# A float16 score pass over 64 rows widened to 128 with zeros, the weight split taken off GpSimd, and a new order

## The chip, the cores and the metric

The kernel runs on one core of one Trainium2 chip. The metric is the device time of one execution in microseconds; the kernel before has a median of 1103.67 us over 3 runs (1102.92 to 1103.91). The engines have short names in the profile: PE is the matrix engine and PEld its weight loads, DVE is VectorE, ACT is ScalarE, POOL is GpSimd, SP is the engine whose queue issues the DMAs.

## The reference

Block-causal attention over 8 batches of 8 heads (576 tokens, head size 64), then a feed-forward layer on the 4,608 tokens with 512 features, 2,048 hidden. All arrays are float32.

```python
scores = scale * np.matmul(q, k.transpose(0, 1, 3, 2))
mask = block_i >= block_j                  # blocks of 64 tokens
scores = np.where(mask, scores, -1000000000.0)
scores = scores - np.max(scores, axis=-1, keepdims=True)
attn = np.exp(scores)
attn = attn / (np.sum(attn, axis=-1, keepdims=True) + 1e-09)
out = np.matmul(attn, v)
...
h = x @ w_in
g = np.maximum(0.01 * h, h)
return (g @ w_out).astype(np.float32)
```

## The kernel before, in words

**Precision.** To reach float32 accuracy at the speed of 16-bit matmuls, an operand is split into a high half (the value scaled by a power of two and rounded to float16) and a low half (what is left over). A product then takes several matmuls that add up in one accumulator. The powers of two come from sums of squares: one per weight matrix, one per group of four heads for v and for q and k, one per stretch of x.

**Stages.** `work` lists 80 pieces of attention. Batch 0 comes as 8 "lo" and 8 "hi" pieces with float32 matmuls, while both weight matrices are loaded, their squares summed and then split; batch 1 comes as 8 "first" and 8 "rest" pieces; all further heads are "full". From batch 3 on (`SB = 3`), 40 heads in all, the scores are computed in float16 (`sixteen`). The feed-forward work goes by 18 chunks of 256 tokens, each with 8 units of two matmul groups: `ffn1` (line 989, 24 matmuls a unit, result through ScalarE's leaky step and split into `gh` and `gl`) and `ffn2` (line 1007, 12 matmuls a unit). A chunk becomes available when the attention of its tokens is done.

**The float16 scores** (lines 537 to 551 and 590 to 595). q and k of a head lie in `qk_in` with 128 rows: the 64 features and, below, the 64 features again in reverse roles. Four steps make the operands. ScalarE or VectorE writes `sx2`, the scaled high half of k, and the upper half of `sx1`, the high half of q. VectorE's line 546 writes `sx3`, what `sx2` left over; its upper 64 rows are the low half of k, its lower 64 rows the low half of q. Two DMAs of 72 KB each on SP, both within the on-chip memory, bring q's low half under q's high half (line 549) and k's high half a second time under itself (line 550). The first matmul pass, over 128 rows, then multiplies q's high and low halves by k's high half at once; the second, over 64 rows, multiplies q's high half by k's low half:

```python
nc.tensor.matmul(
    ap, sx1[0:64, cols] if c else sx1[:, cols], sx3[0:64, k0:k1] if c else sx2[:, k0:k1], start=first, stop=last
)
```

A head has two blocks of such matmuls at line 591. The first has the query tiles in the order (3, 0), (0, 0), (3, 1), (0, 1), (2, 0), (1, 0), (2, 1), (1, 1), where the second number is the pass; their widths are 448, 64, 448, 64, 320, 192, 320 and 192 columns. The second block, for tile 4, has two matmuls of pass 0 and two of pass 1, 288 columns each. The maxima (line 622), the exponentials (line 639), the split of the probabilities (lines 682 and 686), their transposes by DMA (line 693) and the values (line 809) follow. The buffers of a head alternate between two sets, so a head's operands can be made while the head before is at work, but not before the scores two heads back are done.

**The weight split** (`weight_split`, lines 464 to 486). When all 16 pieces of a matrix are loaded and the scale is known, each piece of 128 x 512 gets a high half by ScalarE, VectorE or GpSimd and a low half by VectorE or GpSimd. GpSimd takes two instructions for a low half (lines 475 and 476).

**What sets the order.** Nothing is scheduled on the chip. `Plan` is a list scheduler that runs while the kernel is built: every operation has a rank, mostly in units of one head, one or more engines with a cost in ns for each, and the buffers that it reads and writes. The planner replays time with those costs, gives each free engine the ready operation of the lowest rank, and the instructions are emitted in that order. On the chip every engine, SP's queue included, runs its own list in order and waits where an operand is not there. The constants of lines 39 to 84 shift the ranks: `OFF1`, `OFF2`, `SL1` and `AHEAD` place the weight pieces and their loads, `LEAD` and `LAG` the feed-forward units behind the attention, `RP` the making of a head's operands, `RN` the split of the probabilities. `HOLD` and `HOLDP` are delays after which the second choice of engine is considered. `fill` puts dummy matmuls on PE in the first stage.

Of the kernel before, what the change touches and what calls it, by code (L numbers as in the profile page):

```python
# [12 lines left out]
F16 = mybir.dt.float16  # L13
BF16 = mybir.dt.bfloat16
AF = mybir.ActivationFunctionType
ALU = mybir.AluOpType
# [6 lines left out]
S = 576  # L23
# [12 lines left out]
GROUP = 4  # L36
AHEADV = 3
AHEADQ = 5
RW = -0.799

RL = 4.591
RP = -0.92
RB = 0.202
RT = 2.998
RV = 2.189
RX = -6.219
RN = -1.606

LEAD = 3.83
LAG = 1.993  # L50
RS = 2.699
RG = 0.188
OFF1 = 4.299
OFF2 = -4.211
SL1 = 12.694
AHEAD = -2.515

LAT = 1550
HOLDP = 475.817
HOLD = 186.808  # L60
FILL = 235
FILLTO = 12
# [12 lines left out]
TISSUE, TMOVE = 1230, 125  # L75
SLOW = 8000
SIDE = 34
STEPA = 0.586
STEPB = 0.594
VD = 4.394  # L80
JOINT = 0
SB = 3
RQ = 3.331
RD = 0.704


class Plan:
# [148 lines left out]
def dma(size):  # L236
    return size / 360


def pool2(n):  # L240
    return n * 2.14 + 168


def pool1(n):
    return n * 0.83 + 240
# [3 lines left out]
def attention_ffn(ctx: ExitStack, tc: tile.TileContext, qk0: bass.AP, qk: bass.AP, v: bass.AP, w_in: bass.AP, w_out: bass.AP, out: bass.AP):  # L249
    nc = tc.nc  # L250
# [10 lines left out]
    add = plan.add  # L261
# [67 lines left out]
    ptf = fixed([P, 1024], F32, "ptf")  # L329
# [36 lines left out]
    def carve(y, shape, dt):  # L366
        size = 1
        for n in shape:
            size *= n
        words = size // (1 if dt == F32 else 2)  # L370
        ap = slab[y][:, used[y] : used[y] + words].bitcast(dt)
        used[y] += words
        if len(shape) == 1:
            return ap
        names = "abcd"[: len(shape)]
        return ap.rearrange(f"p ({' '.join(names)}) -> p {' '.join(names)}", **dict(zip(names[1:], shape[1:])))
# [4 lines left out]
    xr[1] = carve(0, [ND, S], F32)  # L381
    ob[1] = carve(0, [DM], F32)
    xh[1], xl[1] = (carve(1, [ND, CH], F16) for _ in range(2))
    qk16 = [carve(y, [3, S], F16) for y in range(2)]
    prow = [prow, [carve(1, [pw[t]], F32) for t in range(NT)]]

    def powers(e, s, i):
# [76 lines left out]
    def weight_split(rank, f, out_side):  # L464
        w, y = WIDE, 1 if out_side else 0
        if out_side:
            hi, lo = woh[:, f], wol[:, f]
        else:
            hi, lo = (x[:, f].rearrange("p c f -> p (c f)") for x in (wih, wil))
        key, v_key = ("wo" if out_side else "wi", f), ("val", out_side, f)  # L470
        val = slab[y][:, f * WIDE : (f + 1) * WIDE].bitcast(F32)
        by = ws[:, y : y + 1]

        def twice():
            nc.gpsimd.tensor_scalar(val, val, by, 1.0, op0=ALU.mult, op1=ALU.mult)
            nc.gpsimd.tensor_sub(lo, val, hi)  # L476

        add([
            ("ACT", act(w, True) + 93, lambda: nc.scalar.mul(hi, val, by)),
            ("POOL", pool1(w), lambda: nc.gpsimd.tensor_scalar(hi, val, by, 1.0, op0=ALU.mult, op1=ALU.mult)),  # L480
            ("DVE+", dve(w, True), lambda: nc.vector.tensor_scalar_mul(hi, val, by)),
        ], rank, [v_key, ("ws", y)], [(key, 0)])
        add([
            ("DVE+", dve(w) + 62, lambda: nc.vector.scalar_tensor_tensor(lo, val, by, hi, op0=ALU.mult, op1=ALU.subtract)),
            ("POOL", pool1(w) + pool2(w), twice),
        ], rank, [v_key, (key, 0), ("ws", y)], [(key, 1), v_key])

    def attention(i):
        n, kind = work[i]
        b, h = divmod(n, H)  # L490
        z = i % 2
# [3 lines left out]
        qkt, qkey = qk_in[z], ("qkt", z)  # L495
# [38 lines left out]
        rp = r0 - RP  # L534
        if plain_s:
            qkd = [qkey]
        elif sixteen:
            eq, kq = divmod(n - SB * H, GROUP)
            sx1, sx2, sx3 = (qk16[z][:, y] for y in range(3))
            c = 2 * GROUP * eq + kq  # L540
            mine, cross = later["qsc"][:, c : c + 1], later["qsc"][:, c + GROUP : c + GROUP + 1]
            esc = later["qx"][:, GROUP * eq + kq : GROUP * eq + kq + 1]
            k1, k2, k3 = (("x", z, y, "q") for y in range(3))
            add(copying(S, lambda: sx2, lambda: qkt[:, 1], by=cross), rp, [qkey, ("qsc", eq)], [k2])
            add(copying(S, lambda: sx1[0:64], lambda: qkt[0:64, 0], by=mine[0:64]), rp, [qkey, ("qsc", eq)], [k1])
            add([("DVE+", dve(S) + 120, lambda: nc.vector.scalar_tensor_tensor(
                sx3, qkt[:, 1], cross, sx2, op0=ALU.mult, op1=ALU.subtract
            ))], rp, [qkey, ("qsc", eq), k2], [k3])
            add([("SP", 475, lambda: nc.sync.dma_start(sx1[64:128], sx3[64:128]))], rp, [k3], [k1], lag=dma(S * 64 * 2))
            add([("SP", 475, lambda: nc.sync.dma_start(sx2[64:128], sx2[0:64]))], rp, [], [k2], lag=dma(S * 64 * 2))  # L550
            qkd = [k1, k2, k3]
        else:
            qd, khd, kld = qs[z][:, qa:qe], kk[z][:, 0, :ke], kk[z][:, 1, :ke]
            add(copying(qe - qa, lambda: qd, lambda: q_in, by=eighth[:, 0:1]), rp, [qkey], [("qs", z)])
            add(copying(ke, lambda: khd, lambda: k_in, by=eighth[:, 1:2]), rp, [qkey], [("kh", z)])
            add(subtracting(qe - qa, lambda: qd[64:128], lambda: q_in[64:128], lambda: qd[64:128]), rp, [qkey], [("qs", z)])
            add(subtracting(ke, lambda: kld[0:64], lambda: k_in[0:64], lambda: khd[0:64]), rp, [qkey, ("kh", z)], [("kl", z)])
            qkd = [("qs", z), ("kh", z), ("kl", z)]
        if not plain_v:
            e, k = divmod(n - H, GROUP)  # L560
            vkey, by, back = ("vr", e % 2, k), vsc[:, e : e + 1], vin[:, e : e + 1]
# [17 lines left out]
        def scores(tiles):  # L579
            banks = [bank for bank, _ in tiles]  # L580
            for y, (b, (t, ap, k0, k1, c)) in enumerate(tiles):
                first, last = b not in banks[:y], b not in banks[y + 1 :]
                cols = slice(q0[t], q0[t] + P)
                if plain_s:
                    go = lambda ap=ap, cols=cols, k0=k0, k1=k1, first=first, last=last: nc.tensor.matmul(
                        ap, q_in[:, cols.start - qa : cols.stop - qa], k_in[:, k0:k1], start=first, stop=last
                    )
                    yield 4 * RATE * (k1 - k0), go, LOADS
                    continue
                if sixteen:  # L590
                    go = lambda ap=ap, cols=cols, k0=k0, k1=k1, c=c, first=first, last=last: nc.tensor.matmul(  # L591
                        ap, sx1[0:64, cols] if c else sx1[:, cols], sx3[0:64, k0:k1] if c else sx2[:, k0:k1], start=first, stop=last
                    )
                    yield RATEH * (k1 - k0), go, LOADH
                    continue
                if c == 2:
                    go = lambda ap=ap, cols=cols, k0=k0, k1=k1, first=first, last=last: nc.tensor.matmul(
                        ap, qs[z][:, cols], kk[z][:, :, k0:k1], start=first, stop=last
                    )
                    yield 2 * RATE * (k1 - k0), go, LOADS  # L600
                    continue
                go = lambda ap=ap, cols=cols, c=c, k0=k0, k1=k1, first=first, last=last: nc.tensor.matmul(
                    ap, qs[z][:, cols], kk[z][:, c, k0:k1], start=first, stop=last
                )
                yield RATE * (k1 - k0), go, LOADS
# [129 lines left out]
        for base, c0, w, items in tgroups.get(kind, ()):  # L735
            x = bank()
# [7 lines left out]
            hi = ptf[:, base : base + w]  # L744
# [141 lines left out]
    def q_group(e):  # L886
# [4 lines left out]
        if e == 0:  # L891

            def blocks():
                for ap, x in ((same, 0), (other, 64)):
                    nc.gpsimd.memset(ap, 0.0)
                    nc.gpsimd.memset(ap[0:64, x : x + 64], 1.0)
                    nc.gpsimd.memset(ap[64:128, 64 - x : 128 - x], 1.0)

            add([("POOL", 1200, blocks)], rank - 2, [], [("ptf", 0), ("ptf", 512), "blocks"])
        for k in range(GROUP):  # L900
            y = (GROUP * e + k) % 3
            buf, key = q_raw[y], ("qn", y)
# [137 lines left out]
    for i in range(len(work) + 1):  # L1040
        if i == 2 * H:

            def second(y):
                nc.gpsimd.memset(parts[y], 0.0)

            for y in range(2):
                new = [("ph", y, t, k) for t in range(NT) for k in (0, 1)] + [("pt", y, t) for t in range(NT)]
                new += [("p", 1, t) for t in range(NT)] + [(a, 1, d) for a in ("xh", "xl") for d in range(0, CH, BLK)] if y else [("x", 1, h, k) for h in range(H) for k in range(3)] + [("ob", 1)]
                new += [("x", y, k, "q") for k in range(3)]
                kind = "wo" if y else "wi"  # L1050
                add([("POOL", 2500, lambda y=y: second(y))], 0, [("val", bool(y), f) for f in range(NF)], new)
        if i in events:
# [63 lines left out]
```

## Time and profile before

| | |
|---|---|
| median of 3 runs | 1103.67 us |
| the profiled execution | 1104.85 us, span 1103.0 us |
| mean granted clock of PE | 0.986 |
| PE busy | 1064.6 us (97%) |
| VectorE, ScalarE, GpSimd busy | 64%, 66%, 16% |
| line 591, score matmuls in float16 | 480 matmuls, 349.7 to 922.0 us |
| DMAs from `slab` to `slab`, 72 KB each | 80 |

The profile shows one execution. A group row names line, engine, operation, output<-inputs, shapes and count; then busy us, the mean ns of one, and the engine's idle time before the group with what ended it. A timeline row begins with start and length in us; `[x <-y]` at its end is idle time before it and the releaser. Rows of stages give the stretch, its length, busy us and instruction counts of PE, PEld, DVE, ACT and POOL (of those that have any), the granted clock as a share of full speed, the busy share of the DMA engines and GB/s. Matmuls are pipelined: a matmul's printed length overlaps the next, so what a run of matmuls takes is read from start to start. SPq is SP's queue of DMA issues.

### The profile page before, as it was taken

How to read it: one execution, taken by the hardware profiler on the slowest of the kernel's cores; microseconds unless marked ns; L12 is line 12 of the kernel's file. 1: busy time of each engine (PE TensorE's matmuls, PEld its weight loads, DVE VectorE, ACT ScalarE, POOL GpSimd, SP SyncE). 2: the span in 40 equal slices, each digit the busy share in tenths (PEclk: the TensorE clock that was granted, in tenths of full speed). 3: DMA queues.
4: the chain of work that ended last, by engine and by line, in shares of the span. 5: the costliest groups of instructions: out<-in, count | busy, mean ns of one | idle time of the engine just before them, and what ended most of it. 6: DMA issues, size and time to landing. Idle time of an engine off the chain costs nothing.

```text
span 1103.0 us, 22107 instructions
## 1 busy us (share of the span) xinstructions
PE 1064.6 (97%) x8374; PEld 737.4 (67%) x8374; DVE 702.6 (64%) x1861; ACT 723.9 (66%) x1687; POOL 181.1 (16%) x224
## 2 busy tenths in 40 slices
PE   9999799998897899999999999999999999999998
PEld 7887466676664566666666666666666666766665
DVE  4687556888888777786866576676666765221111
ACT  5888546777886777786766577788767765322222
POOL 1010610431442210222100002211121210000000
PEclk9999899999999799999999999999999999999999
DMA  7856235798789787778884756878776754000000
GB/s 267 269 172 235 70 90 110 133 203 185 183 195 219 165 184 159 150 160 194 151 171 83 168 150 135 166 166 176 127 169 126 144 86 92 1 20 4 17 21 19
DMA packets 263178, 152.56 MB, mean 138 GB/s; under 512 B 223648, under 2 KB 240032, under 8 KB 263072
## 3 DMA queue, kind: packets, MB, share of 16 engines
q1 hardware_dynamic: 263072, 151.16, 59.7%
q8 instruction: 65, 1.06, 0.4%
q14 instruction: 41, 0.34, 0.1%
HBM read 80.74 MB, written 9.44 MB: 82 GB/s over the span
## 4 chain that ended last, share of the span: by engine, by line
PE 66%; DVE 1%; DMA 1%; ACT 0%; issue 0%; SPq 0%; DVEq 0%
PE p_h L989 27%; PE p_o L1007 26%; PE p_s L591 6%; PE p_t L809 5%; DMA slab<-slab 1%; PE p_t L952 0%; PE p_t L913 0%; DVE nm L622 0%; PE p_t L880 0%; ACT prow L639 0%; DVE slab L686 0%; DVE xl L973 0%; DVE xh L969 0%; DVE slab L1023 0%; ACT slab L1022 0%
## 5 line engine op out<-in xcount | busy, mean ns | idle before, releaser
L989 PEld LDWEIGHTS <-wih 128*128 128x128 f16 x2304 | 222.0, 99 | 74.4 <-issue 10.9
L994 ACT ACTIVATE g<-p_h 128x512 f32<-128x512 f32 x144 | 85.5, 594 | 176.4 <-PE p_h L989 172.3
L989 PE MATMUL p_h<-slab,wih 128*128 128x256 f16 x1152 | 197.2, 273 | 0.1
L1007 PE MATMUL p_o<-wol,gh 128*128 128x512 f16 x576 | 172.4, 381 | 5.6 <-POOL wol L476 5.6
L1007 PE MATMUL p_o<-woh,gh 128*128 128x512 f16 x576 | 172.9, 382 | 0.0
L1007 PE MATMUL p_o<-woh,gl 128*128 128x512 f16 x576 | 172.3, 381 | 0.0
L1007 PEld LDWEIGHTS <-gh 128*128 128x128 f16 x1152 | 109.3, 100 | 85.2 <-issue 5.8
L989 PE MATMUL p_h<-xh,wih 128*128 128x256 f16 x576 | 158.7, 276 | 2.9 <-DVE xh L969 2.9
L989 PE MATMUL p_h<-xl,wih 128*128 128x256 f16 x576 | 158.5, 275 | 1.0 <-DVE xl L973 1.0
L989 PE MATMUL p_h<-xh,wil 128*128 128x256 f16 x576 | 158.4, 275 | 0.0
L989 PE MATMUL p_h<-slab,wil 128*128 128x256 f16 x576 | 157.4, 273 | 0.0
L275 DVE TENSOR_TENSOR gl<-g,gh 128x512 bf16<-128x512 f32 x94 | 64.6, 688 | 145.4 <-ACT gh L265 122.5
L622 DVE TENSOR_REDUCE nm<-p_s 128x1 f32<-128x192 f32 (+4 forms) x308 | 138.6, 485 | 8.1 <-ACT prow L639 2.6
L989 PEld LDWEIGHTS <-wil 128*128 128x128 f16 x1152 | 113.3, 98 | 15.3 <-issue 1.6
L1007 PEld LDWEIGHTS <-gl 128*128 128x128 bf16 x576 | 56.6, 98 | 74.3 <-issue 7.0
L276 POOL TENSOR_TENSOR gl<-g,gh 128x512 bf16<-128x512 f32 x50 | 62.6, 1253 | 245.9 <-ACT gh L265 166.0
L809 PEld LDWEIGHTS <-vs 128*128 128x128 f16 x1680 | 86.0, 99 | 15.2 <-issue 9.8
L809 PE MATMUL p_t<-slab,vs 128*128 128x128 f16 (+1 forms) x1680 | 91.1, 212 | 3.4 <-DVE slab L686 1.9
L591 PE MATMUL p_s<-slab 128*128 128x448 f16 (+2 forms) x480 | 85.1, 281 | 5.0 <-ACT prow L639 2.8
L686 DVE SCALAR_TENSOR_TENSOR slab<-slab,rec 128x192 f16<-128x192 f32 (+4 forms) x140 | 76.8, 571 | 9.0 <-ACT slab L682 8.5
L686 DVE SCALAR_TENSOR_TENSOR slab<-prow,rec,slab 128x192 f16<-128x192 f32 (+4 forms) x140 | 74.4, 554 | 9.9 <-ACT slab L682 9.4
L613 DVE MEMSET p_s<- 64x64 f32 (+1 forms) x196 | 24.7, 126 | 87.6 <-PE p_s L591 55.2
(163 smaller groups left out, 1578.8 us busy)
## 6 DMA issues: line engine op xcount, KB each, us to landing
qk_in<-in_qk SPq DMA_DIRECT2D x56, 576.0 KB, 4.9
raw<-in_qk SPq DMA_DIRECT2D x40, 288.0 KB, 3.6
raw<-in_w_in SPq DMA_DIRECT2D x16, 512.0 KB, 4.6
raw<-in_w_out SPq DMA_DIRECT2D x16, 512.0 KB, 4.7
slab<-slab SPq DMA_DIRECT2D x80, 72.0 KB, 4.5
out<-ob SPq DMA_DIRECT2D x18, 256.0 KB, 2.3
out<-slab SPq DMA_DIRECT2D x18, 256.0 KB, 2.0
v_raw<-in_v SPq DMA_DIRECT2D x7, 640.0 KB, 5.3
```

Source lines behind the costliest of these rows:

```text
L275: ("DVE+" if sb else "DVE", dve(n) + 100, lambda: nc.vector.tensor_sub(dst(), one(), two())),
L276: ("POOL", pool2(n) - (0.25 * n if n == 512 else 0), lambda: nc.gpsimd.tensor_sub(dst(), one(), two())),
L591: go = lambda ap=ap, cols=cols, k0=k0, k1=k1, c=c, first=first, last=last: nc.tensor.matmul(ap, sx1[0:64, cols] if c else sx1[:, cols], sx ...
L613: nc.vector.memset(ap, NEG)
L622: [("DVE", dve(kw[t]), lambda t=t, ap=ap, flat=flat: nc.vector.tensor_reduce(nm[z][: qn[t], t : t + 1], ap[: qn[t]], axis=AX.X if flat els ...
L686: ("DVE+", dve(w) + 62, lambda: nc.vector.scalar_tensor_tensor(part(1), p, by, part(0), op0=ALU.mult, op1=ALU.subtract)),
L809: nc.tensor.matmul(p_t[x][:, c : c + src.free_size()], vs[z][:, (j + 1) % NT], src, start=start, stop=stop)
L989: nc.tensor.matmul(hh[:, i, :], w[:, f, d, :], x[:, d, :], start=k == 0, stop=k == len(terms) - 1)
L994: add([("ACT", act(512), lambda: nc.scalar.activation(g[z], hh, AF.Prelu, alpha=0.01, scale=DOWN))], rank, [("h", z)], [("g", z)])
L1007: nc.tensor.matmul(p_o[m], a[:, i, m * P : (m + 1) * P], w[:, 2 * u + i, :], start=u == 0 and k == 0, stop=u == NU - 1 and k == 5,)
```

## The change

The subtraction writes a fourth tile, `sx4`. A third DMA of the same size brings its upper 64 rows, k's low half, to `sx3[0:64]`; the lower 64 rows of `sx3` are set to zero once by GpSimd, for both sets of buffers, in the operation that also prepares the block matrices for the scales. The second pass multiplies all 128 rows of `sx1` by `sx3`, so that q's low half meets zeros. The scores' matmuls wait for all three DMAs. GpSimd is no longer a choice for either half of the weights. Nineteen of the planner's constants have other values; `LAG`, `RL`, `RS`, `HOLD`, `FILL` and the planner's costs are as before.

```diff
-RW = -0.799
+RW = -0.819
...
-RP = -0.92
-RB = 0.202
-RT = 2.998
-RV = 2.189
-RX = -6.219
-RN = -1.606
-
-LEAD = 3.83
+RP = -1.361
+RB = 0.283
+RT = 1.774
+RV = 2.243
+RX = -5.633
+RN = -1.756
+
+LEAD = 4.283
...
-RG = 0.188
-OFF1 = 4.299
-OFF2 = -4.211
-SL1 = 12.694
-AHEAD = -2.515
+RG = 0.245
+OFF1 = 4.515
+OFF2 = -4.38
+SL1 = 16.003
+AHEAD = -0.135
...
-HOLDP = 475.817
+HOLDP = 475.007
...
-STEPA = 0.586
-STEPB = 0.594
-VD = 4.394
+STEPA = 0.659
+STEPB = 0.675
+VD = 4.498
...
-RQ = 3.331
-RD = 0.704
+RQ = 3.122
+RD = 1.397
...
-    qk16 = [carve(y, [3, S], F16) for y in range(2)]
+    qk16 = [carve(y, [4, S], F16) for y in range(2)]
...
-        def twice():
-            nc.gpsimd.tensor_scalar(val, val, by, 1.0, op0=ALU.mult, op1=ALU.mult)
-            nc.gpsimd.tensor_sub(lo, val, hi)
-
         add([
             ("ACT", act(w, True) + 93, lambda: nc.scalar.mul(hi, val, by)),
-            ("POOL", pool1(w), lambda: nc.gpsimd.tensor_scalar(hi, val, by, 1.0, op0=ALU.mult, op1=ALU.mult)),
             ("DVE+", dve(w, True), lambda: nc.vector.tensor_scalar_mul(hi, val, by)),
         ], rank, [v_key, ("ws", y)], [(key, 0)])
         add([
             ("DVE+", dve(w) + 62, lambda: nc.vector.scalar_tensor_tensor(lo, val, by, hi, op0=ALU.mult, op1=ALU.subtract)),
-            ("POOL", pool1(w) + pool2(w), twice),
         ], rank, [v_key, (key, 0), ("ws", y)], [(key, 1), v_key])
...
             add([("DVE+", dve(S) + 120, lambda: nc.vector.scalar_tensor_tensor(
-                sx3, qkt[:, 1], cross, sx2, op0=ALU.mult, op1=ALU.subtract
-            ))], rp, [qkey, ("qsc", eq), k2], [k3])
-            add([("SP", 475, lambda: nc.sync.dma_start(sx1[64:128], sx3[64:128]))], rp, [k3], [k1], lag=dma(S * 64 * 2))
+                sx4, qkt[:, 1], cross, sx2, op0=ALU.mult, op1=ALU.subtract
+            ))], rp, [qkey, ("qsc", eq), k2], [k4])
+            add([("SP", 475, lambda: nc.sync.dma_start(sx1[64:128], sx4[64:128]))], rp, [k4], [k1], lag=dma(S * 64 * 2))
             add([("SP", 475, lambda: nc.sync.dma_start(sx2[64:128], sx2[0:64]))], rp, [], [k2], lag=dma(S * 64 * 2))
+            add([("SP", 475, lambda: nc.sync.dma_start(sx3[0:64], sx4[0:64]))], rp, [k4], [k3], lag=dma(S * 64 * 2))
             qkd = [k1, k2, k3]
...
                 if sixteen:
                     go = lambda ap=ap, cols=cols, k0=k0, k1=k1, c=c, first=first, last=last: nc.tensor.matmul(
-                        ap, sx1[0:64, cols] if c else sx1[:, cols], sx3[0:64, k0:k1] if c else sx2[:, k0:k1], start=first, stop=last
+                        ap, sx1[:, cols], (sx3 if c else sx2)[:, k0:k1], start=first, stop=last
                     )
...
+                for y in range(2):
+                    nc.gpsimd.memset(qk16[y][64:128, 2], 0.0)
+
-            add([("POOL", 1200, blocks)], rank - 2, [], [("ptf", 0), ("ptf", 512), "blocks"])
+            add([("POOL", 1200, blocks)], rank - 2, [], [("ptf", 0), ("ptf", 512), "blocks", ("x", 0, 2, "q"), ("x", 1, 2, "q")])
```

More of the change, by code (lines that the diff above doesn't have):

```diff
@@ L538, in attention @@
             eq, kq = divmod(n - SB * H, GROUP)
-            sx1, sx2, sx3 = (qk16[z][:, y] for y in range(3))
+            sx1, sx2, sx3, sx4 = (qk16[z][:, y] for y in range(4))
             c = 2 * GROUP * eq + kq
@@ L542, in attention @@
             esc = later["qx"][:, GROUP * eq + kq : GROUP * eq + kq + 1]
-            k1, k2, k3 = (("x", z, y, "q") for y in range(3))
+            k1, k2, k3, k4 = (("x", z, y, "q") for y in range(4))
             add(copying(S, lambda: sx2, lambda: qkt[:, 1], by=cross), rp, [qkey, ("qsc", eq)], [k2])
@@ L1048, in attention_ffn @@
                 new += [("p", 1, t) for t in range(NT)] + [(a, 1, d) for a in ("xh", "xl") for d in range(0, CH, BLK)] if y else [("x", 1, h, k) for h in range(H) for k in range(3)] + [("ob", 1)]
-                new += [("x", y, k, "q") for k in range(3)]
+                new += [("x", y, k, "q") for k in range(4)]
                 kind = "wo" if y else "wi"
```

## The prediction

> **What bounds the kernel now.** I read the page's head first, then a table of busy time by stage, then the matrix engine's own timeline and its waits.
>
> ```profile
> span 1103.0 us, 22107 instructions
> ...
> PE 1064.6 (97%) x8374; PEld 737.4 (67%) x8374; DVE 702.6 (64%) x1861; ACT 723.9 (66%) x1687; POOL 181.1 (16%) x224
> ```
>
> The stages, with PE, PEld, DVE, ACT and POOL busy, then the granted clock, DMA share and GB/s:
>
> ```profile
> 0.00:120.00 120.00, 117.81 (x886) 96.50 (x887) 86.26 (x235) 95.06 (x224) 12.34 (x32) 1.00 0.69 233
> 120.00:150.00 30.00, 24.41 (x119) 13.32 (x118) 13.96 (x37) 13.14 (x34) 17.32 (x13) 0.89 0.11 28
> 150.00:262.00 112.00, 109.85 (x896) 80.42 (x894) 85.45 (x226) 77.26 (x189) 28.77 (x29) 1.00 0.72 148
> 262.00:375.00 113.00, 90.00 (x740) 64.18 (x740) 96.62 (x260) 85.03 (x215) 35.37 (x43) 0.91 0.85 193
> 375.00:922.00 547.00, 545.30 (x4487) 363.12 (x4483) 384.85 (x1047) 401.31 (x944) 87.01 (x110) 1.00 0.71 149
> 922.00:1103.00 181.00, 177.19 (x1258) 119.88 (x1256) 35.48 (x60) 52.10 (x86) 0.32 (x1) 1.00 0.07 21
> ```
>
> From 375 us on, PE is idle for 1.7 of 547 us and then only at the end, while VectorE and ScalarE are busy 70 and 73%. In that stretch whatever PE stops doing comes off the end. The real holes are two: 120 to 150 us, with 5.6 us idle and a clock of 0.89, and 262 to 375 us, with 23.0 us idle and 0.91.
>
> **The full-row second pass.** The 40 float16 heads run two blocks of score matmuls each (line 591): eight matmuls, then four. Beside them stands a block of 30 value products (line 809), all over 128 rows.
>
> ```profile
> 571.56 1.35 PE L591 MATMUL p_s<-slab 128*128 128x448 f16 x8
> 572.84 0.39 PE L989 MATMUL p_h<-slab,wih 128*128 128x256 f16 x2
> ...
> 578.06 1.57 PE L809 MATMUL p_t<-slab,vs 128*128 128x64 f16 x30
> 579.47 0.76 PE L591 MATMUL p_s<-slab 128*128 128x288 f16 x4
> 580.16 0.39 PE L989 MATMUL p_h<-slab,wih 128*128 128x256 f16 x2
> ```
>
> Start to start is what a block costs, since the printed length overlaps the next. By the code, the value block streams 3,200 columns (20 matmuls of 128, 10 of 64); it takes 579.47 - 578.06 = 1.41 us, or 0.441 ns a column, with a new weight load for each. The eight score matmuls stream 2 x (448 + 64 + 320 + 192) = 2,048 columns, which at that rate is 0.90 us; they take 572.84 - 571.56 = 1.28 us, 0.38 too much. The four stream 4 x 288 = 1,152, worth 0.51 us, and take 0.69, 0.18 too much. Where does it go? The weight loads of the first block show it:
>
> ```profile
> 571.34 0.31 PEld L591 LDWEIGHTS <-slab 128*128 128x128 f16 x2
> 571.87 0.11 PEld L591 LDWEIGHTS <-slab 64*128 64x128 f16 x2 [0.21 <-issue]
> 572.19 0.11 PEld L591 LDWEIGHTS <-slab 128*128 128x128 f16 x2 [0.21 <-issue]
> 572.51 0.11 PEld L591 LDWEIGHTS <-slab 64*128 64x128 f16 x2 [0.21 <-issue]
> 572.84 0.11 PEld L989 LDWEIGHTS <-wih 128*128 128x128 f16 x2 [0.21 <-issue]
> ```
>
> The loader pauses each time the number of rows changes, 128 to 64 and 64 to 128, and not between equals. That makes four changes in the block of eight and two in the block of four: 0.38/4 = 95 ns and 0.18/2 = 90 ns a change, the same price twice. With 128 rows in both passes there is no change left. The columns stay as many, so the zeros cost nothing by the value block's rate. How many heads lie where this counts:
>
> ```profile
> 349.00:375.00 26.00, 5.11 (x24) 1.78 (x24) 0.74 0.89 204
> 375.00:922.00 547.00, 79.74 (x456) 31.24 (x456) 1.00 0.71 149
> ```
>
> 456 of the 480 matmuls, 38 heads, run where PE has no slack: 38 x (0.38 + 0.18) = 21.3 us. Two heads lie in a stage where PE also waits for others; I count nothing for them, and the upper bound is 40 x 0.56 = 22.4.
>
> The Trainium skill ("TensorE: Matmul & The Clock Gate", Part 3: Packing small matmuls) speaks against this: it says a weight load overlaps a running matmul only when the row groups differ. The trace disagrees, since the 30 loads of the value block, all on the same 128 rows, cost nothing.
>
> **The third copy.** SP issues two small copies per head now. The rows are those of two heads, the landing times, and PE's one wait for them:
>
> ```profile
> 558.45 0.59 SPq L550 DMA_DIRECT2D slab<-slab  x1
> ...
> 569.76 0.59 SPq L550 DMA_DIRECT2D slab<-slab  x1
> ```
>
> ```profile
> L550 SPq DMA_DIRECT2D slab<-slab x40: 467/587/695, 343.3 to 900.7; - x40
> DMA to landing us min/median/max: 2.1/4.4/7.2
> ```
>
> ```profile
> PE p_s L591 <- DMA slab<-slab: 1.7, 1, 1.7
> ```
>
> The copy issued at 558.45 feeds the block at 571.56, so it lands at about 562.9, 8.7 us early. A third behind it starts 0.59 us later and still lands some 8 us early. Queued behind it on SP are that head's neighbours' transposes and loads, each 0.59 us later. One head of 40 waited (1.7 us); it would wait 0.6 more. Its own conditions are those of the first copy (the same subtraction, the same scores two heads back), so SP does not newly wait. I take 0; the bounds are 0 and 0.6 us for each of 40 heads, 24 us, were SP's order the limit everywhere. Below zero it cannot go: it adds work only. The subtraction now writes a fourth tile, which frees VectorE from waiting for old scores; the same instruction, 0. The two zero fills on GpSimd, once, resemble this row and by their ranks lie ahead of the first float16 head, 0:
>
> ```profile
> 3.50 0.57 POOL L321 MEMSET kk<- 64x576 f32 x1
> ```
>
> **No GpSimd in the weight split.** GpSimd now does four low halves and one high half. This is the burst after the last weight piece:
>
> ```profile
> 120.54 7.35 POOL L475 TENSOR_SCALAR slab<-slab,ws 128x512 f32<-128x512 f32 x1
> 127.97 1.15 POOL L476 TENSOR_TENSOR wol<-slab,woh 128x512 f16<-128x512 f32 x1
> 129.10 0.69 POOL L475 TENSOR_SCALAR slab<-slab,ws 128x512 f32<-128x512 f32 x1
> ```
>
> ```profile
> 120.62 6.70 DVE L484 SCALAR_TENSOR_TENSOR wol<-slab,ws,woh 128x512 f16<-128x512 f32 x10
> ```
>
> ```profile
> 122.78 0.59 PE L1007 MATMUL p_o<-woh,gh 128*128 128x512 f16 x2
> 123.21 0.38 PE L1007 MATMUL p_o<-wol,gh 128*128 128x512 f16 x1
> 129.17 0.59 PE L1007 MATMUL p_o<-wol,gh 128*128 128x512 f16 x1 [5.58 <-POOL wol L476]
> ```
>
> A scaling that takes 0.69 us alone took 7.35 while VectorE ran ten splits without a pause, and ended 0.6 us after the last. PE stood 5.58 us for one low half. The Trainium skill ("SBUF — State Buffer", SBUF: two separate sides) calls the port that the two engines share an exclusive lock; this agrees. Then the clock, by the last but two number:
>
> ```profile
> 129.00:130.00 1.00, 0.83 (x3) 0.28 (x3) 0.00 (x0) 0.00 (x0) 0.92 (x3) 0.50 0.00 0
> 133.00:134.00 1.00, 1.00 (x4) 0.42 (x3) 0.00 (x0) 0.00 (x0) 1.00 (x1) 0.50 0.00 0
> 134.00:135.00 1.00, 1.00 (x6) 0.39 (x4) 0.00 (x0) 0.00 (x0) 0.26 (x1) 0.82 0.00 0
> ```
>
> From 129.17 to about 134.4, 5.2 us of matmuls ran at half clock, so 2.6 us were lost. Together 5.58 + 2.6 = 8.2 us. What replaces it: VectorE does three more splits in this burst at 6.70/10 = 0.67 us, 2.0 us. PE's pass over a pair of pieces has 12 matmuls, 2.6 us by the first two rows (two matmuls in 0.43), and needs two splits, 1.34 us; VectorE stays ahead and I take none of the 2.0. Behind it VectorE sits idle anyway:
>
> ```profile
> 137.53 0.30 DVE L613 MEMSET p_s<- 64x64 f32 x2 [10.08 <-PE p_s L585]
> ```
>
> PE is then next to continuously busy to 262 us, so the 8.2 us pass on. Bounds: 8.2, and 6.2 if the extra splits were on the path.
>
> **The order.** Nineteen constants of the planner move. By the code, the load of the first weight piece gets rank 5.15 instead of 7.21 and that of the last 20.65 instead of 19.51; preparing a float16 head is 0.44 of a head later, the feed-forward 0.45 later. No row prices this. It cannot gain from 375 us on, where PE has no holes; what it can touch are the holes before. Bounds: half of the 23.0 idle us of 262 to 375 gone, 11.5 us, or one more stall like the 8.2 us one and half as much again, 12 us. Nothing says which, so 0.
>
> **Sum.** The profiled execution took 1104.85 us (span 1103.0, 1.85 around it): 1104.85 - 21.3 - 8.2 = 1075.3. The median of the runs is 1.18 lower, 1103.67, so 1074.2, said as 1074.
>
> **Rivals.** (1) The new order closes holes: 1074 - 12 = 1062. For it: from 262 to 375 us PE, VectorE and ScalarE are busy 80, 86 and 75%, none of them full. Against: each head's chain of scores, exponentials, transposes and values stays as it is. (2) The new order opens a hole: 1074 + 12 = 1086. [...] (3) The loss is the loader's own, not the change of rows, so the passes gain nothing: 1103.67 - 8.2 = 1095.5. Against it: the loads without a pause between equal rows. (4) Slower: the third copy ends last. It decides from the point where it lands over 8 us later than I place it, for instance behind a transpose that SP holds; every microsecond beyond that is paid by each of 38 heads, and from 29.5/38 = 0.8 us on it eats the gain. At 1 us it gives 1074 + 38 = 1112. Against it: one wait in 40 now. (5) Every load of full rows waits for the running matmul as the changes do now, 12 waits a head for 6: 1103.67 - 8.2 + 38 x 6 x 0.094 = 1117. Against it: the value block's 30 loads. This is what the page named above in the Trainium skill would have.
>
> **Numbers.** Forecast 0.60, (1) 0.17, (2) 0.15, (3) 0.03, (4) 0.03, (5) 0.02. Leaving out the last three and the outer edges of (1) and (2), the range is 1061 to 1087. This kernel's measurement can tell about 0.2%, 2.2 us, from no change. Faster: all but (4) and (5), 0.94 after 0.01 for ending level; slower 0.05.
>
> **What would show it.** In the changed profile: line 591 has 480 matmuls of 128 rows, the blocks start to start 0.90 and 0.50 us, the loader without pauses of 0.2; no GpSimd under the splits and no wait of line 1007 for it; PEclk without the dip near 130 us; from the start of the float16 heads to the last some 21 us shorter; the tail's 181 us unchanged. Wrong if the blocks still take 1.28 us, if line 591 waits for the small copies in many heads, or if the idle time before 375 us differs by over 12 us.

## The result, and the profile after

The changed kernel takes 1073.12 us (median of 5 runs, 1072.22 to 1074.84) against 1103.67: a ratio of 0.972, with a 95% interval of 0.9701 to 0.974. The forecast was 1074. Its profiled execution took 1072.31 us, span 1070.2.

The same stages as before the change, with busy us of PE, PEld, DVE, ACT and POOL, the granted clock, the DMA share and GB/s:

```profile
0.00:120.00 120.00, 116.41 (x867) 94.82 (x868) 87.52 (x239) 95.15 (x225) 5.59 (x26) 1.00 0.69 233
120.00:150.00 30.00, 29.77 (x180) 18.67 (x178) 19.55 (x67) 16.98 (x47) 8.56 (x10) 1.00 0.19 48
150.00:262.00 112.00, 107.69 (x883) 77.82 (x881) 86.89 (x223) 79.28 (x186) 27.76 (x28) 1.00 0.72 159
262.00:375.00 113.00, 91.80 (x763) 68.39 (x764) 95.77 (x259) 83.13 (x207) 38.78 (x46) 0.88 0.86 186
375.00:922.00 547.00, 545.61 (x4684) 392.57 (x4683) 388.62 (x1048) 402.72 (x951) 92.15 (x121) 1.00 0.74 156
922.00:1070.00 148.00, 143.96 (x985) 96.08 (x982) 22.70 (x32) 38.29 (x62) 0.00 (x0) 1.00 0.04 15
```

Two rows differ in kind. From 120 to 150 us PE is now busy for 29.77 of 30 us, where it was 24.41, and the clock is 1.00, not 0.89. From 375 to 922 us PE is as full as it was, but 4,684 matmuls fit where 4,487 did. The hole from 262 to 375 us is as it was: 21.2 idle us and a clock of 0.88.

PE's timeline at two score blocks (line 591 is line 586 now, 602 is 597, 809 is 804, 1007 is 1004):

```profile
573.31 0.65 PE L586 MATMUL p_s<-slab 128*128 128x288 f16 x4
573.80 0.38 PE L1004 MATMUL p_o<-woh,gh 128*128 128x512 f16 x1
...
585.88 1.04 PE L586 MATMUL p_s<-slab 128*128 128x448 f16 x8
586.75 1.57 PE L804 MATMUL p_t<-slab,vs 128*128 128x64 f16 x30
```

And the loads of the block of eight, from the timeline of PEld:

```profile
585.66 0.97 PEld L586 LDWEIGHTS <-slab 128*128 128x128 f16 x8
586.67 0.29 PEld L804 LDWEIGHTS <-vs 128*128 128x128 f16 x5
```

Start to start the blocks take 0.49 and 0.87 us, where they took 0.69 and 1.28. The eight loads are one row without a pause inside it, where four rows each began with 0.21 us of idle time.

PE's waits that bear on the prediction:

```profile
PE p_s L597 <- ACT prow L634: 7.2, 7, 1.7
PE p_s L597 <- ACT slab L634: 6.7, 4, 3.0
PE p_t L804 <- DMA slab<-slab: 4.3, 3, 2.8
PE p_s L586 <- ACT prow L634: 2.6, 1, 2.6
```

The wait of 5.6 us for GpSimd's low half has no row any more, and line 586 has none for a DMA: no head waits for the small copies. The waits for ScalarE's exponentials, 12.4 us before at the float32-type scores (the two rows of line 602 together), are 13.9. From 262 to 375 us they are 10.4 of the 21.2 idle us, 11.9 of 23.0 before: about half of the hole that stays. The rest of it is spread over shorter waits for DMAs, ScalarE and VectorE.

### The profile page after: what moved, and what is told of

Its sections match the earlier page's. It is cut to its first block, busy times and chain, and to the rows that moved or that the text cites. A ratio compares the mean times of both kernels' runs of the same rounds, so it can differ in the third digit from the quotient of the medians.

```text
span 1070.2 us, 22133 instructions
## 1 busy us (share of the span) xinstructions
PE 1035.2 (97%) x8352; PEld 748.3 (70%) x8352; DVE 701.0 (66%) x1863; ACT 715.5 (67%) x1676; POOL 172.8 (16%) x231
## 4 chain that ended last, share of the span: by engine, by line
PE 65%; DMA 2%; DVE 0%; ACT 0%; issue 0%; SPq 0%
PE p_h L986 27%; PE p_o L1004 27%; PE p_t L804 5%; PE p_s L586 5%; DMA slab<-slab 1%; DMA raw<-in_qk 1%; PE p_t L949 0%; PE p_t L910 0%; ACT prow L634 0%; DVE nm L617 0%; DVE xl L970 0%; PE p_t L875 0%; DVE xh L966 0%; DVE slab L681 0%; ACT slab L1019 0%
## 5 line engine op out<-in xcount | busy, mean ns | idle before, releaser
L986 PEld LDWEIGHTS <-wih 128*128 128x128 f16 x2304 | 224.4, 99 | 70.1 <-issue 2.9
L681 DVE SCALAR_TENSOR_TENSOR slab<-prow,rec,slab 128x448 f16<-128x448 f32 (+4 forms) x140 | 74.8, 560 | 14.0 <-ACT slab L677 13.3
L586 PE MATMUL p_s<-slab 128*128 128x448 f16 (+2 forms) x480 | 69.4, 282 | 4.4 <-ACT prow L634 2.6
L265 ACT CAST gh<-g 128x512 f16<-128x512 f32 x112 | 68.9, 615 | 2.5
```

The costliest lines, as they stand in the source:

```text
L265: one = lambda: nc.scalar.copy(dst(), src())
L986: nc.tensor.matmul(hh[:, i, :], w[:, f, d, :], x[:, d, :], start=k == 0, stop=k == len(terms) - 1)
```

## The experiments

Two theories were at stake. Mine: the gain is 21 to 23 us from six changes of rows a head at some 95 ns each, and 8 us from GpSimd's late low half; the third copy and the order bring nothing. The rivals: the price lies in each 64-row matmul and not in the change; the order is the real gain; the third copy takes something back; the hole only moves. The runs are put beside the kernel before on the same chip (1102.4 to 1104.4 us) and beside the changed kernel's 1073.12. These medians of the kernel before lie 2 us apart, so a difference of under 2 us from the changed kernel is not resolved.

### The second pass over 64 rows again, all else as changed

```diff
-    ap, sx1[:, cols], (sx3 if c else sx2)[:, k0:k1], start=first, stop=last
+    ap, sx1[0:64, cols] if c else sx1[:, cols], sx3[0:64, k0:k1] if c else sx2[:, k0:k1], start=first, stop=last
```

> The changed kernel with the second score pass over 64 rows again; the third copy is still issued and awaited, and every engine's order of instructions is the changed kernel's. Theory (a change of rows between neighbouring matmuls costs PE some 95 ns, six changes a head): the blocks at the score line take 1.28 and 0.69 us again, the time is 23 us above the changed kernel, about 1096 us. Rival (the gain came from the order): within 2 us of the changed kernel, 1073. Rival (half and half): about 1085.

1094.03 us (ratio to before 0.9928, 0.9899 to 0.9956), 20.9 us above the changed kernel. PE's timeline has the old blocks:

```profile
574.67 1.35 PE L586 MATMUL p_s<-slab 128*128 128x448 f16 x8
575.95 1.58 PE L804 MATMUL p_t<-slab,vs 128*128 128x64 f16 x30
...
581.29 0.76 PE L586 MATMUL p_s<-slab 128*128 128x288 f16 x4
581.98 0.60 PE L1004 MATMUL p_o<-woh,gh 128*128 128x512 f16 x2
```

1.28 and 0.69 us again. No engine's order changed, so the rows alone are worth these 21 us. The blocks would give 38 x (0.41 + 0.20) = 23.2 us, which is what was expected; the other 2 us are not placed.

### The 64-row matmuls side by side

```diff
-    "full": ((3, 0), (0, 0), (3, 1), (0, 1), (2, 0), (1, 0), (2, 1), (1, 1)),
+    "full": ((3, 0), (0, 0), (2, 0), (1, 0), (3, 1), (0, 1), (2, 1), (1, 1)),
```

> The kernel with 64 rows in the second pass, and in the block of eight the four matmuls of the first pass stand before the four of the second, so the block has two changes of rows and not four; the block of four keeps its two. Theory (the price is per change of rows): the block of eight takes 1.28 - 2 x 0.095 = 1.09 us, the time is 38 to 40 x 0.19 = 7.5 us below the kernel with 64 rows in the old sequence, about 1088 us. Rival (the price is per matmul over 64 rows, four in the block either way): 1.28 us and no difference, 1096.

1088.42 us (ratio 0.9862, 0.9843 to 0.988), 5.6 below the ungrouped one (the spans differ by 1091.7 - 1084.8 = 6.9). The timeline of PE:

```profile
572.61 1.14 PE L586 MATMUL p_s<-slab 128*128 128x448 f16 x8
573.68 1.58 PE L804 MATMUL p_t<-slab,vs 128*128 128x64 f16 x30
...
579.02 0.76 PE L586 MATMUL p_s<-slab 128*128 128x288 f16 x4
579.71 0.60 PE L1004 MATMUL p_o<-woh,gh 128*128 128x512 f16 x2
```

The block of eight takes 1.07 us, the block of four is as it was. Four 64-row matmuls are still there; two changes of rows are gone, and with them 1.28 - 1.07 = 0.21 us. The remaining two cost 1.07 - 0.87 = 0.20. So the price, about 0.1 us, belongs to the change and not to the matmul. The 5.6 us are less than the 38 x 0.21 = 8.0 of the blocks; the difference is not placed. A kernel that cannot fill the rows could have had a quarter to a third of the gain by a resorted list.

### Without the third copy

```diff
-            add([("SP", 475, lambda: nc.sync.dma_start(sx3[0:64], sx4[0:64]))], rp, [k4], [k3], lag=dma(S * 64 * 2))
+            add([("SP", 475, lambda: None)], rp, [k4], [k3], lag=dma(S * 64 * 2))
...
-                    nc.gpsimd.memset(qk16[y][64:128, 2], 0.0)
+                    nc.gpsimd.memset(qk16[y][:, 2], 0.0)
```

With the upper rows of `sx3` zeroed once as well, the second pass adds nothing: this kernel leaves out q by k's low half.

> The changed kernel without the third copy, all other instructions in the same order; the second pass multiplies by zeros, so the product of q with the low half of k is left out. Theory (the third copy lies beside other work): within 2 us of the changed kernel, 1071 to 1075. Rival (the third copy delays SP's queue and through it the transposes or the scores): 3 to 10 us below the changed kernel.

1071.65 us (1070.75 to 1072.54), 1.5 below the changed kernel's median, ratios 0.9712 (0.9694 to 0.973) and 0.972 (0.9701 to 0.974): no difference that these runs resolve. The rival of 3 to 10 us is out.

### GpSimd out of the weight split, in the old order

```diff
-            nc.gpsimd.tensor_scalar(val, val, by, 1.0, op0=ALU.mult, op1=ALU.mult)
-            nc.gpsimd.tensor_sub(lo, val, hi)
+            nc.vector.scalar_tensor_tensor(
+                lo, val, by, hi, op0=ALU.mult, op1=ALU.subtract)
```

The one high half goes to VectorE in the same way.

> The kernel before, with the five pieces of the weight split that GpSimd does issued on VectorE at the same places of the order; PE, ScalarE and SP have the same instructions in the same order. Theory (the GpSimd scaling is starved while VectorE runs splits, PE waits 5.6 us and then runs 5.2 us at half clock): the wait and the dip near 130 us are gone, 8 us below the kernel before, about 1095.5; 6 us if the extra splits on VectorE are on the path. Rival (the hole is only moved, since the next stage waits for attention): within 2 us of the kernel before, 1103.

1095.86 us (ratio 0.9932, 0.9915 to 0.9949): 8.2 us less than the 1104.07 of the kernel before beside it, or 7.5 by the ratio, against the forecast's term of 8.2. Its stages around the burst, and VectorE's ten splits:

```profile
120.00:127.00 7.00, 7.00 (x35) 3.37 (x34) 6.95 (x13) 7.00 (x14) 2.13 (x1) 1.00 0.00 0
127.00:135.00 8.00, 8.00 (x43) 4.70 (x42) 5.55 (x18) 2.93 (x13) 1.16 (x1) 1.00 0.19 49
```

```profile
122.02 6.70 DVE L484 SCALAR_TENSOR_TENSOR wol<-slab,ws,woh 128x512 f16<-128x512 f32 x10
```

PE is never idle from 120 to 135 us, at full clock, though VectorE reaches the ten splits 1.4 us later than before. The extra splits were not on the path.

### The order alone, the pass alone, both parts without the order

The first is the kernel before with the nineteen new constants. The second is the full-row pass with the constants of before and GpSimd in the split. The third is the changed kernel with the constants of before:

```diff
...
-OFF1 = 4.515
-OFF2 = -4.38
-SL1 = 16.003
-AHEAD = -0.135
+OFF1 = 4.299
+OFF2 = -4.211
+SL1 = 12.694
+AHEAD = -2.515
...
```

> The kernel before with the changed kernel's nineteen constants alone; GpSimd may still take weight pieces and by this order takes other ones (five low halves of the first matrix, one high half of the second). Theory (the order in itself is worth little; what it can touch are the holes before 375 us, chiefly the one at 123 to 134 us): between 1092 and 1106, nearer to 1095 if the second matrix's low halves no longer go to GpSimd, since that takes the 8 us hole away by another road. Rival (the order is the main gain): 1085 or less.

> The full-row second pass with its third copy, with the constants of before and GpSimd still in the weight split (its share is the same pieces as before). Theory (the parts add up): the pass is worth 21 to 23 us, the hole near 123 us stays, 1081 to 1083. Rival (without the new order the third copy makes waits): above 1086.

> The changed kernel with all nineteen constants of before. Theory (the order is worth nothing beside the two other parts): 1072 to 1076, as the changed kernel. Rival (the order closes holes before 375 us): 1080 or more. Rival (it opens them): 1068 or less.

The order alone took 1095.86 us (ratio 0.9923, 0.9903 to 0.9944), the pass alone 1080.79 (0.9787, 0.9769 to 0.9805), pass and split without the order 1074.23 (0.9724, 0.9702 to 0.9747). The last two add up: 23.6 us against the 1104.38 of the kernel before beside them, then 6.6 more, and the order's own share of the changed kernel is the 1.1 us from 1074.23 to 1073.12, which is not resolved. In the kernel with the pass alone the old wait stands in PE's list as it was (line 1007 is 1010 there):

```profile
PE p_o L1010 <- POOL wol L476: 5.6, 1, 5.6
```

Yet the order alone brought 8.5 us. Its GpSimd shows why; line 476 now makes `wil` and no `wol`. VectorE's splits beside it follow:

```profile
67.21 1.47 POOL L476 TENSOR_TENSOR wil<-slab,wih 128x512 f16<-128x512 f32 x1
70.28 1.41 POOL L475 TENSOR_SCALAR slab<-slab,ws 128x512 f32<-128x512 f32 x1 [1.60 <-ACT nm L632]
```

```profile
66.52 8.37 DVE L484 SCALAR_TENSOR_TENSOR wil<-slab,ws,wih 128x512 f16<-128x512 f32 x8
```

By this order GpSimd splits pieces of the first matrix, some 55 us before the hole, and none of the second but one high half. So the wait for its low half is gone here too, and the order and the removal of GpSimd do not add. But the hole is not closed. The stages of the burst with the order alone:

```profile
120.00:127.00 7.00, 4.66 (x27) 3.10 (x27) 4.71 (x21) 3.98 (x11) 1.69 (x7) 1.00 0.64 179
127.00:135.00 8.00, 7.37 (x34) 3.31 (x34) 7.97 (x17) 7.97 (x17) 3.01 (x1) 1.00 0.25 87
```

PE is idle for 2.34 + 0.63 = 3.0 us, at full clock, where the kernel before lost 5.6 us of waiting and 2.6 of half clock: 5.2 of the 8.2 us are gone. The scale of the second matrix (line 389) is written at 124.82 us, 8 us later than in the changed kernel (116.78), and 1.7 of the 3.0 us are waits for that matrix's halves. What brought the other 3.3 of the 8.5 us is not settled. The profile of the kernel before has one more wait of PE, 1.7 us for a small copy at line 591, with 1.7 us of half clock behind it, and that of the order alone has neither. But the kernel with the small clearings, further down, has neither as well, in the old order, and is no faster than the kernel before.

### The changed kernel with GpSimd back in the split

```diff
...
             ("ACT", act(w, True) + 93, lambda: nc.scalar.mul(hi, val, by)),
+            ("POOL", pool1(w), lambda: nc.gpsimd.tensor_scalar(hi, val, by, 1.0, op0=ALU.mult, op1=ALU.mult)),
...
+            ("POOL", pool1(w) + pool2(w), twice),
```

> The changed kernel with GpSimd again a choice in the weight split; by this order it takes five low halves of the first matrix and one high half of the second, and no low half of the second. Theory (the hole of 8 us came from the second matrix's low halves, and the new order has none of them on GpSimd): within 3 us of the changed kernel, 1071 to 1076. Rival (GpSimd in the split costs wherever it stands, since it also slows VectorE's splits beside it): 1078 to 1082.

1076.72 us, 3.6 above the changed kernel: between the two. The stages of the burst:

```profile
120.00:127.00 7.00, 4.72 (x28) 3.10 (x27) 4.70 (x21) 3.98 (x11) 0.72 (x1) 1.00 0.62 182
127.00:135.00 8.00, 7.35 (x26) 2.97 (x26) 7.97 (x17) 7.97 (x17) 2.93 (x1) 0.79 0.24 84
```

No low half is late from GpSimd, but a smaller hole has come back: 2.28 + 0.65 = 2.9 idle us and a clock of 0.79 from 127 to 135 us. It is the hole of the order alone: PE has the same waits there, and the scale of the second matrix is written at 124.87 us. In both kernels the planner, with GpSimd as a choice, issues the last loads of that matrix from 110 us on; in the changed kernel the last of them are issued from 102.65 us. What differs is the clock: full with the order alone, here 0.50 to 0.52 from 129 to 132 us, which costs some 1.5 us more.

### No third copy at all

```diff
-                sx4, qkt[:, 1], cross, sx2, op0=ALU.mult, op1=ALU.subtract
-            ))], rp, [qkey, ("qsc", eq), k2], [k4])
-            add([("SP", 475, lambda: nc.sync.dma_start(sx1[64:128], sx4[64:128]))], rp, [k4], [k1], lag=dma(S * 64 * 2))
+                sx3, qkt[:, 1], cross, sx2, op0=ALU.mult, op1=ALU.subtract
+            ))], rp, [qkey, ("qsc", eq), k2], [k3])
+            add([("SP", 475, lambda: nc.sync.dma_start(sx1[64:128], sx3[64:128]))], rp, [k3], [k1], lag=dma(S * 64 * 2))
...
-            add([("SP", 475, lambda: nc.sync.dma_start(sx3[0:64], sx4[0:64]))], rp, [k4], [k3], lag=dma(S * 64 * 2))
```

> The changed kernel with no third copy and no fourth tile: the subtraction writes the operand of the second pass itself, and its lower rows hold q's low half where the zeros were, so that the sum takes in q's low half by q's low half. The planner makes its order anew. Theory (the third copy costs nothing): 1071 to 1076, the spread being the new order's. Rival (it costs SP and DMA time): 1069 or less. Rival (VectorE now waits for the scores two heads back before it may subtract): 1078 or more.

1072.03 us (1070.23 to 1072.12; ratio 0.9706, 0.9687 to 0.9724). Neither rival: it is level with the changed kernel, with 40 DMAs fewer and the fourth tile unused. The zeros are there for the meaning of the sum, not for the time.

### What lets GpSimd in

The forecast said that the scaling starves "while VectorE ran ten splits without a pause". Two runs put something between the splits of the kernel before: the first one column cleared ahead of every low half, the second 1,280 columns of 16 bits once, after the first of the ten.

```diff
...
-            ("DVE+", dve(w) + 62, lambda: nc.vector.scalar_tensor_tensor(lo, val, by, hi, op0=ALU.mult, op1=ALU.subtract)),
+            ("DVE+", dve(w) + 62, lambda: (nc.vector.memset(pause, 0.0), nc.vector.scalar_tensor_tensor(lo, val, by, hi, op0=ALU.mult, op1=ALU.subtract))),
```

> The kernel before with a clearing of one column (some 0.1 us) put on VectorE ahead of each low half of the weight split; GpSimd keeps its five pieces, and all engines keep their order. Theory (GpSimd's scaling gets in as soon as VectorE does anything else than a split): the scaling that took 7.35 us takes under 2 us, PE's wait of 5.6 us for it and the half clock behind it are gone or nearly, 6 to 8 us below the kernel before, 1096 to 1098. Rival (it waits out the ten splits in any case): the scaling takes over 7 us and the time is that of the kernel before or 1 us more, 1104.

```diff
-            ("DVE+", dve(w) + 62, lambda: nc.vector.scalar_tensor_tensor(lo, val, by, hi, op0=ALU.mult, op1=ALU.subtract)),
+            ("DVE+", dve(w) + 62, lambda: (nc.vector.memset(junk, 0.0) if out_side and f == 5 else None, nc.vector.scalar_tensor_tensor(lo, val, by, hi, op0=ALU.mult, op1=ALU.subtract))),
```

> The kernel before with one longer clearing (1,280 columns of 16 bits, 0.3 to 0.7 us) on VectorE between the first and the second of the ten splits in the burst; GpSimd keeps its pieces, all orders stay. The clearings of 0.06 us each did not let GpSimd in. Theory (an instruction that reads nothing, long enough, does): the scaling that took 7.35 us ends some 1 to 3 us after it began, the low half that PE waits for is there by 125 us and not 129.2, PE waits under 2 us, the half clock is gone; 5 to 8 us below the kernel before, 1095 to 1098. Rival (GpSimd waits until VectorE has nothing left in its queue): the scaling again takes 7 to 8 us, 1104.

Both theories fell. The ratios are to the kernel before on the same chip, 1102.39 and 1103.58 us. With the small clearings the kernel takes 1102.64 us (ratio 1.0004, 0.9995 to 1.0013), with the one long clearing 1104.47 (1.0009, 0.9994 to 1.0025), and the scaling is as late as ever. GpSimd and VectorE with the small ones:

```profile
120.93 7.44 POOL L475 TENSOR_SCALAR slab<-slab,ws 128x512 f32<-128x512 f32 x1
```

```profile
121.01 0.74 DVE L484 SCALAR_TENSOR_TENSOR wol<-slab,ws,woh 128x512 f16<-128x512 f32 x1
121.02 0.06 DVE L484 MEMSET pause<- 128x1 f32 x1
121.68 0.74 DVE L484 SCALAR_TENSOR_TENSOR wol<-slab,ws,woh 128x512 f16<-128x512 f32 x1
```

And with the long one:

```profile
120.70 7.87 POOL L475 TENSOR_SCALAR slab<-slab,ws 128x512 f32<-128x512 f32 x1
```

```profile
120.77 0.73 DVE L484 SCALAR_TENSOR_TENSOR wol<-slab,ws,woh 128x512 f16<-128x512 f32 x1
121.59 0.59 DVE L484 MEMSET junk<- 128x640 uint32 x1
122.10 5.91 DVE L484 SCALAR_TENSOR_TENSOR wol<-slab,ws,woh 128x512 f16<-128x512 f32 x9
127.94 0.21 DVE L658 RECIPROCAL rec<-rec 128x1 f32<-128x1 f32 x2
```

A small clearing begins 0.01 us after a split and runs inside it, so it is no pause at all. The long one stands by itself for 0.5 us, and still GpSimd ends only after the last split (128.57, against 128.01). That fits a GpSimd that waits until VectorE has nothing more to do, but a counterexample stands above: in the kernel with the order alone the same scaling took 1.41 us at 70.28, in the midst of eight splits. What differs there is not settled.

## Why the prediction was right

**The pass.** The mechanism held in each of its steps: the pauses of the loader, the price per change of rows (by the grouped run), no cost of the zeros. Rival (5), by which full-row loads would wait as well, is out: the eight loads run without a pause. By the blocks the forecast of 21.3 us was 1.9 us too small. The mis-sized term is the rate of 0.441 ns a column, taken from the value block. The full-row blocks measure 0.87/2,048 = 0.425 and 0.49/1,152 = 0.425 ns, so a head saves 0.41 + 0.20 us and 38 heads 23.2 us. That the value block's rate is higher because its 30 matmuls are short is likely, but no run separates it. The times do not decide between 21.3 and 23.2: with the rows alone undone it was 20.9, with the pass alone in the old order 23.6 against the 1104.38 beside it.

**GpSimd.** 8.2 us was forecast; in the old order 7.5 to 8.2 were measured, with its two halves, the idle PE and the half clock, both gone. That the number came out so close is in part luck. The 2.6 us of half clock were read from one execution: in the profile of the pass alone the same wait of 5.6 us was followed by 1.4 us of it (7.0 together), and there taking GpSimd out gained 6.6. That the extra splits cost nothing held as well. The reason given for the starving held only as far as the trace it was read from: VectorE's splits and GpSimd's lateness go together there, but what ends the wait was not understood.

**The third copy.** Zero, as forecast, to within what the runs resolve.

**The order.** Zero was the value taken because nothing in the profile priced it. In the changed kernel that is what it was (1.1 us, not resolved), and neither rival, 12 us up or down, came. But the step that called it worthless from 375 us on and unpriced before missed two things that it does while GpSimd is a choice: it moves GpSimd's pieces, which ends the wait of 5.6 us without the other edit, and it brings the second matrix's scale 8 us later, and a hole of 3.0 us stays. On its own it is worth 8.5 us. The sum was right because the split without GpSimd removes the same wait, so the two gains overlap instead of adding; that was not foreseen.

**The tail.** Here one step of the list of signs failed. It had the stretch from the first float16 score to the last some 21 us shorter and the tail of 181 us unchanged. The score line of the changed kernel, and that of the changed kernel with the old constants (span 1073.2), from the views of that line:

```profile
L586 PE MATMUL p_s<-slab x480: 190/286/562, 340.1 to 883.6; 128*128 128x448 f16 x40, 128*128 128x64 f16 x40, 128*128 128x320 f16 x40, 128*128 128x288 f16 x40
```

```profile
L586 PE MATMUL p_s<-slab x480: 190/286/562, 345.2 to 892.3; 128*128 128x448 f16 x40, 128*128 128x64 f16 x40, 128*128 128x320 f16 x40, 128*128 128x288 f16 x40
```

Before, it ran from 349.7 to 922.0, 572.3 us, with 181.0 behind. After, 543.5 us with 1070.2 - 883.6 = 186.6 behind; with the old constants 547.1 and 180.9. So the stretch is 28.8 us shorter, not 21, and the new constants put 5.7 us of feed-forward work from under the attention behind it. PE is nearly full in both places, so the end hardly moves. With the old constants the stretch is still 25.2 us shorter, since the first float16 score begins only 4.5 us earlier (345.2 against 349.7) and not the 8 us that GpSimd's term would give; where the rest of these went is not shown.

## What to carry to other kernels

On a full PE, read a block of matmuls from start to start and divide by its columns; where two blocks differ, look at the loader's pauses. Neighbouring matmuls over unequal numbers of rows cost PE about 0.1 us a change here, so either sort them by rows or fill the rows up, which is free as long as the columns stay the same. Before adding up the gains of an edit and of a new order, see whether both remove the same wait. And do not take the half clock behind a wait, as read from one execution, for a fixed price: here the same wait of 5.6 us had 2.6 us of it behind it in one kernel and 1.4 in another.

## What the runs showed of the hardware

A 128 x 512 scaling on GpSimd that takes 0.69 us alone took 7.34 to 7.87 us beside ten VectorE splits in four kernels, ending 0.6 us after the last, and neither a 0.06 us nor a 0.59 us clearing between them shortened it; in another order it took 1.41 us among splits, and there the splits grew, to 8.37/8 = 1.05 us from 6.70/10 = 0.67. PE's wait for the low half behind that scaling, 5.6 to 6.1 us, was followed by half clock in all four, at different cost: 2.6 us more behind 5.6 us in the kernel before, 1.4 behind 5.6 with the pass alone. Shorter waits had it behind them too, but not always. One of 1.7 us in the profile of the kernel before, ending at 501.7 us, was followed by a clock of 0.50 from 503 to 506 us and 0.80 in the next. The 3.0 idle us of 120 to 135 us, in pieces of under 1 us, had no half clock behind them with the order alone; nearly the same 2.9 us with GpSimd back in the split had three microseconds of it, some 1.5 us of loss.
